# A written-out emission order made anew, with quarter matmuls side by side

## The chip, the cores and the metric

The program runs on one core of a Trainium2 chip. The metric is the device time of one execution in microseconds (us); lower is better. The engines of the core run side by side, each through its own list of instructions in order: PE (TensorE matmuls; PEld is its weight loads), DVE (VectorE), ACT (ScalarE), POOL (GpSimd), and SP (SyncE), which here issues every DMA.

## What is computed

The reference, cut to its core: attention with keys and values averaged over groups of eight tokens, then a gated MLP whose gate mixes tokens. There are 8 batches of 8 heads, 576 tokens and 64 channels a head; the model has 512 channels and a hidden width of 1024.

```python
k_p = k.reshape(B, H, 72, 8, D).mean(axis=3)
v_p = v.reshape(B, H, 72, 8, D).mean(axis=3)
scores = scale * q @ k_p.transpose(0, 1, 3, 2)
attn = softmax(scores)                       # over 72 pooled keys
x = (attn @ v_p) -> (B, S, H * D)
h = relu(x @ w_in); u, v = h[..., :512], h[..., 512:]
v_n = (v - mean(v)) / sqrt(var(v) + 1e-6)
v_s = einsum('ts,bsd->btd', w_spatial, v_n) + b_spatial[:, None]
out = (u * v_s) @ w_out
```

## The kernel before

Everything is done batch by batch, and every batch is cut into named steps. Attention has K and V (load and pool keys and values), KT (transpose the pooled keys), W (split the left-over pooled values into two parts), Q0 to Q3 (load and transpose the queries of a pair of heads), S0 to S3 (scores and softmax of such a pair), T0, T1, Y0, Y1 (move the probabilities so that pooled keys lie on partitions; Y is the last 64 tokens), and A00 to A11 (probabilities times values: the first digit is a half of the tokens, the second a half of the heads). The MLP has v0 to v4 (one token tile of the gate's input, with its normalisation), u00 to u13, s00 to s13 (token mixing and gating) and o0 to o4 (output projection). w steps load and split the weights. All operands of the large matmuls are split into a high and a low part, so each product takes three matmuls.

The scores (line 612) and the products with the values (line 751) are quarter matmuls: 64 rows by 64 columns of the array, four of which lie beside one another. The MLP's matmuls (lines 804, 820, 847, 865 to 867, 891) take the whole array. Line 754 adds the left-over values behind line 751.

No queue decides the order at run time. Each step is a Python generator; the string ORDER names a step, and `next` runs it to its next `yield`. A digit is the batch, `^`, `~`, `!` and `%` choose the engines of some operations of a step:

```python
for name in ORDER.split():
    ...
    next(parts[key], None)
```

Every engine, SP included, then works through its instructions in that order. Buffers come from rings: PSUM tiles "mm" and "tp" share one ring of four banks, the scores "s" have two, staging "kv" three. A step that takes a tile waits until the last user of that buffer has released it.

Places that the prediction speaks of: `softmax` (line 572 mx, 574 scaled mx, 588 exponentials on ACT, 595 the division on POOL); `load_f64` (lines 213, 222, 224, 227 on DVE, 230, 245, 247 on POOL), which splits a 64-bit weight block; `att_values` (line 504 vr_s) and `att_values_split` (line 512 vr); `normalise` (785 to 793, with the power at 791 on POOL); `moe_v` (808, 814 vn_l on POOL, 827, 837); `moe_s` (870 g, 876, 879 gT on POOL).

Of the kernel before, what the change touches and what calls it, by code (L numbers as in the profile page):

```python
# [23 lines left out]


ORDER = (
    "0Q1^~ 0Q1 wv3^ wv3 0Q1 wv3 0Q0^~ wv3 0Q0 0Q0 ws1 ws1 wv3 ws1 ws1 ws1 0K~ 0K 0V^ 0K 0K 0K 0K 0K 0S0 0S0 0S1 wv3 "
    "wv3 0S0 0S1 0S0 0S1 0S1 0S1 0K 0S0 0V 0S1 0V 0V 0V 0V 0V wv1 0K wv1 wv1 ws1 0S1 0Q2^ 0Q2 0Q2 0S2~ 0S2 0S0 wo1~ "
    "0W 0Y0 wv1 wv1 wv1 0Y0 0Q3^~ 0Y0 0Y0 0T0! 0T0 0T0 0T0 0T0 wo1 0W 0Q3 0Q3 0T0 0T0 0S2 wo1 1Q1^~ wo1 1K 1Q1 1K "
    "wv0~^ 0S3~ 0S3 1Q0^~ 0S2 1K wv2~ 0A00 0A00 0A00 0A00 0A00 1K 1V^ 1Q1 1V 1K 1K 1Q0 wv1 wv0 1Q0 1K 1S1~ wv0 0S3 "  # L30
    "0A10 0A10 1K 0S3 1S0~ wu2 0A10 0S2 wv0 wv0 0S3 0A10 0A10 wv2 1K wv0 0T1! 0S3 0T1 wv2 0Y1 0T1 0T1 0T1 0T1 0T1 "
    "wv2 0Y1 1S1 0Y1 wo1 wo1 0Y1 1V 1V 0A01 0A01 0A01 0A01 0A01 wv2 wv2 wu2 1V 1V wu3~ wu3 wu2 wu2 wu2 1V wu2 wu2 "
    "wu3 wu3 wu3 0v1 0A11 0v1 0A11 0v1 0A11 wu3 wu0 wu0 0A11 wu0 wu0 wb wb 2K~ wu1~^ 0v0 wu1 0v0 wu0 wu0 0A11 0v3 "
    "0v1 wu1 0v3 0v3 1Q2 0v3 1S0 ws4 0v1 1Q2 ws4 1Q3 0v4 ws4 wu0 ws4 0v2 ws4 ws4 0v0 0v0 1S1 1S1 1S1 2K 1S2~ 1S2 2K "
    "wu1 1Q3 0v4 0v4 1S0 0v0 wu1 wu1 wb 0u12 0v2 1S2 0v0 0v2 1S3 0v4 1S0 0u12 0u03 0v1 0u10 0u10 0u02 0v3 1S0 0u03 "
    "0v3 ws0 1T0! 2K 2K 1T0 0u02 0v2 2K 1S3 1T0 1T0 1T0 1T0 0u11 0v2 ws0 1T0 0v2 ws0 0v4 ws0 2Q0 ws0 2Q0 0v2 0u11 1W "
    "1W 0u13 2KT 2KT 0u00 2KT 0u13 0v4 0v4 0u00 1S3 2Q1 2Q1 ws0 1S3 0v0 2S0~ 1A00 2S0 0v3 0u01 0v1 1A00 1A00 1A00 "
    "1A00 1S1 0u01 1S3 ws3 0v4 0v4 ws3 ws3 1Y0 2S1 ws3 ws3 ws3 wo2~!% 1Y0 1Y0 1S3 0s01 wo2 1Y0 1A10 1A10 ws2 1S2 "
    "0s02 0s01 0s01 1A10 1A10 1A10 1S2 1T1! 1T1 1T1 0s01 0s02 1T1 1T1 1T1 wo2 2Q2 0s00 0s02 0s02 ws2 ws2 1T1 2Q2 "
    "0s03 wo3 ws2 0s03 0s03 2Q3 ws2 ws2 wo2 0s13 2S1 0s12 1S3 2S0 0s03 1Y1! wo2 0s00 wo2 2Q3 2S3 1Y1 1Y1 0s13 1Y1 "  # L40
    "2S1 1A11 0s12 1A11 1A11 1A11 3K! 3K 3K 1A11 1v3 1v3 3K wo2 0s12 3Q1 1A01 2S2 2S2 2S2 1A01 1A01 1A01 3K 0s00 3Q0 "
    "3Q0 wo2 2V! 3K 0s12 2S0 1A01 2S1 2S0 0s11 2S2 0s10 2S1 2S1 0s10 0s10 0s10 3KT wo3 1v0 1v0 wo3 wo3 wo3 wo0 0s13 "
    "2S2 0s11 2T0 2T0 0s11 3Q1 0s11 2T0 1u13 wo0 0s13 2S2 1u00 1u00 3Q2 1v2 wo0 wo0 1v2 1v2 3KT 3KT wo0 wo0 wo0 1v4 "
    "1v0 1u01 1u01 1v0 3S1~ 1v0 2T0 2T0 2T0 4Q0 3S1 1v4 1v4 1v4 1v4 wo3 0s00 wo3 1v2 1v2 2S3 2S3 1u10 1u13 1u03 1u10 "
    "1u03 2S1 2Y0! 2V 2Y0 0o3 2T0 2T0 1v1 2V 2V 2V 2S3 2S3 1v3 1v3 3S1 2Y0 1u12 1v3 0o0 1v3 1v1 1v1 0o0 2S3 1v3 0o0 "
    "3S0~ 1u11 0o3 1u11 1v0 2T1! 0o1 2T1 3Q2 3V~ 2T1 1v1 2T1 1v4 1v1 2V 2Y0 2Y0 2S3 2W 2W 2Y1! 1u12 1v1 2A10 2A10 "
    "2A10 0o1 2A10 2A10 3V 1v2 3V 1u02 2Y1 2A00 2A00 2A00 2T1 2T1 1v4 2A00 2A00 0o2 1v0 1v1 1v4 3S0 1v4 1v2 1s13 "
    "1s13 1s11 1s10 3S2~ 1s11 1s13 2Y1 1s12 3V 3V 3V 3S0 3S0 3S0 4Q0 1s10 1s13 0o1 1u02 3S2 1s00 0o2 2T1 1s12 4K! "
    "0o3 2T1 3S2 1s12 4K 4K 4K 1s12 4K 2A01 2A01 2A01 2A01 1s00 1s10 1s10 2A01 2Y1 2v1 2v1 2Y1 2A11 2A11 2A11 2A11 "
    "3Q3 3Q3 2v0 5K! 3S3 2A11 3T0 2v0 3T0 4K 4KT 1s00 1s00 3S1 3W 2v4 2v4 2v4 4Q1 4V~ 2v4 4V 1s01 4KT 1s01 3S1 1s01 "  # L50
    "3S3 1s02 3S1 1s02 3Y0 3Y0 4KT 3S3 1s11 1s11 1s03 4S0~ 1s03 3S3 3S3 2v1 1s02 2v1 1s02 2v1 1o4 1o4 1o2 3Y0 3S2 "
    "0o2 3S2 3T1 1o4 3W 1o2 2v4 3S3 4V 4V 2v4 4V 3Y0 3Y0 1s03 2u00 2u00 4Q1 4Q3 3T0 4Q2 2v1 2v3 2v3 2v3 2u13 2v3 4V "
    "3T0 3T0 2u11 3T0 4Q2 2v4 2u02 2v0 2v0 3T1 5Q0 2u13 2u11 2u01 2v4 2u12 2u12 4S0 4S0 2u03 2u03 2v1 1s01 4S1~ 4S1 "
    "5V~ 1s03 4S1 1o0 1o0 3T0 5K 1o2 2u01 2u02 1o3 1o3 4Q3 2v0 2v0 2v2 3T0 4S0 4S0 4T0 3T1 4T0 2v0 5K 5K 4S2 3S3 "
    "3Y1! 3T1 3T1 3T1 3A00 3A00 3A00 3A00 4S3 2v2 2v3 4S2 2v3 2v3 3Y1 2v2 2v2 3A00 3A10 2u10 3A10 1o3 2v2 2v2 2v2 "
    "2v4 3A10 3A10 3A10 4S1 4S1 1o1 4S2 2s10 5K 5K 4S2 3T1 2s01 2u10 2s10 2s10 2s10 5Q0 2s11 3Y1 1o0 2s11 2s11 2s02 "
    "5KT 1o1 2s02 6V~ 5Q2 4T0 3Y1 3Y1 2s01 4S1 2s01 4Y0 3T1 2s01 4T0 5KT 2s13 4T0 3A11 5KT 2s13 2s13 2s13 3A11 3A11 "
    "2s03 2s03 3A11 3A11 4S3 4S3 5Q2 3v2 4Y0 4Y0 2s03 3A01 3A01 3A01 3u11 6Q0 4S3 4S3 2s11 3A01 3A01 3v4 3v4 3v4 "
    "2s00 2s00 2s00 2s00 3v2 3v2 2s02 3v2 3v0 3v0 3v0 4S2 4S2 4T1 4S3 2s12 5S2~ 2s03 3v3 3u01 5Q3 5Q3 4W 3v2 2s12 "
# [907 lines left out]
```

## Time and profile before

| | |
|---|---|
| median of 3 runs | 576.53 us (573.49 to 578.07) |
| the profiled execution's own time | 573.28 us |
| its span, first to last instruction | 571.5 us |
| mean granted TensorE clock | 0.988 |
| PE, PEld busy | 94%, 80% of the span |
| DVE, ACT, POOL busy | 58%, 47%, 51% |
| chain that ended last | PE 67%, DVE 15%, ACT 5%, POOL 4%, DMA 4%, issue 3% |

The chain is followed back from the last instruction: at each point it shows the engine that everything behind it waited for. A matmul is shown with its whole passage through the array, so matmuls that follow one another overlap in the profile; what one costs is the distance from its start to the next one's start.

### The profile page before, as it was taken

Reading aid. Unit: us, or ns where it says so; the run is one execution under the profiler, and the core shown is the slowest. Engines: PE = TensorE matmul, PEld = TensorE weight load, DVE = VectorE, ACT = ScalarE, POOL = GpSimd, SP = SyncE. Lnnn points to the kernel's source line nnn. Section 1 sums busy time; section 2 is a strip of 40 time slices with the busy share of each in tenths; the row PEclk is TensorE's granted clock in tenths of the full one; section 3 lists DMA queues with packets and bytes.
Section 4 is the critical chain, followed back from the end, with each engine's and each line's share of the span. In section 5 each row is a group of like instructions: output and inputs, shape, how many; then the busy total and the mean of one; then the engine's idle time right before and its main releaser. Section 6 shows DMA issues by size and latency. Waiting matters only on the chain.

```text
span 571.5 us, 12170 instructions
## 1 busy us (share of the span) xinstructions
PE 538.1 (94%) x4514; PEld 456.3 (80%) x4514; DVE 333.0 (58%) x723; ACT 269.7 (47%) x875; POOL 288.9 (51%) x389
## 2 busy tenths in 40 slices
PE   4879798998999999999999999999999997999997
PEld 3666497887877896888888988988898895888996
DVE  3899999767864655566755655452845464333110
ACT  2675876543555426334564346425445333224231
POOL 2446555689776483834846645271544182132430
PEclk9999999999899999999999999999999998999999
DMA  8887155266167466445434342552134122001002
GB/s 224 244 278 166 46 123 100 81 118 154 48 183 181 120 125 170 149 115 121 115 105 122 111 97 98 115 146 58 62 103 128 44 87 72 24 2 51 24 25 87
DMA packets 124363, 63.13 MB, mean 110 GB/s; under 512 B 82960, under 2 KB 108048, under 8 KB 124304
## 3 DMA queue, kind: packets, MB, share of 16 engines
q1 hardware_dynamic: 124304, 62.36, 41.0%
q8 instruction: 35, 0.57, 0.4%
q14 instruction: 24, 0.20, 0.1%
HBM read 44.92 MB, written 17.40 MB: 109 GB/s over the span
## 4 chain that ended last, share of the span: by engine, by line
PE 67%; DVE 15%; ACT 5%; POOL 4%; DMA 4%; issue 3%; SPq 1%; DVEq 0%; ACTq 0%; POOLq 0%
PE mm L865 16%; PE mm L891 13%; PE mm L804 11%; PE mm L847 11%; PE tp L751 3%; PE s_ps L612 3%; ACT e L588 2%; PE tp L754 2%; PE mm L820 2%; DVE vv L793 1%; PE mm L866 1%; PE mm L867 1%; DVE x L222 1%; DVE vr_s L504 1%; DVE x L213 1%
## 5 line engine op out<-in xcount | busy, mean ns | idle before, releaser
L847 PE MATMUL mm<-xT,win_h 128*128 128x256 f32 (+1 forms) x512 | 104.3, 298 | 0.0
L879 POOL TENSOR_TENSOR gT<-g,gT 128x256 fp32r<-128x256 f32 x64 | 47.9, 753 | 99.0 <-ACT gT L876 91.3
L891 PE MATMUL mm<-wout_h,gT 128*128 128x512 f32 (+1 forms) x264 | 84.1, 401 | 3.2 <-DVE vv L827 2.7
L804 PE MATMUL mm<-win_h,xT 128*128 128x512 f32 x256 | 82.7, 402 | 4.3 <-DVE xT L183 2.4
L847 PEld LDWEIGHTS mm<-xT,win_h 128*128 128x128 f32 x512 | 83.6, 189 | 2.3
L865 PE MATMUL mm<-wT_h,vn_h 128*128 128x256 f32 (+1 forms) x256 | 76.4, 298 | 1.1 <-DVE xT L761 1.1
L847 PE MATMUL mm<-xT,win_l 128*128 128x256 f32 (+1 forms) x256 | 75.7, 296 | 0.0
L865 PE MATMUL mm<-wT_l,vn_h 128*128 128x256 f32 (+1 forms) x256 | 75.4, 295 | 0.0
L865 PE MATMUL mm<-wT_h,vn_l 128*128 128x256 f32 (+1 forms) x256 | 75.3, 294 | 0.0
L595 POOL TENSOR_TENSOR e<-e,rs 128x720 f32<-128x720 f32 (+1 forms) x32 | 41.8, 1305 | 51.9 <-DVE rs L593 46.5
L870 DVE TENSOR_TENSOR g<-mm,ru 128x256 f32<-128x256 f32 (+1 forms) x64 | 28.6, 451 | 62.2 <-PE mm L867 49.2
L891 PEld LDWEIGHTS mm<-wout_h,gT 128*128 128x128 f32 x264 | 49.6, 194 | 15.2 <-issue 2.9
L804 PEld LDWEIGHTS mm<-win_h,xT 128*128 128x128 f32 x256 | 46.6, 189 | 16.5 <-DVE xT L183 3.6
L791 POOL TENSOR_TENSOR rstd<-rstd,neg_half 128x1 f32<-128x1 f32 (+1 forms) x40 | 23.8, 598 | 66.2 <-DVE rstd L789 63.4
L588 ACT ACTIVATE e<-s_ps,mx 128x72 f32<-128x72 f32 x174 | 52.8, 334 | 7.2 <-DVE mx L574 7.0
L891 PE MATMUL mm<-wout_l,gT 128*128 128x512 f32 (+1 forms) x132 | 52.6, 399 | 0.0
L814 POOL TENSOR_TENSOR vn_l<-vv,vn_h 128x512 fp32r<-128x512 f32 x32 | 41.3, 1306 | 21.5 <-ACT vn_h L812 21.5
L804 PE MATMUL mm<-win_l,xT 128*128 128x512 f32 x128 | 50.6, 395 | 0.0
L307 POOL TENSOR_TENSOR st<-st 128x512 f32<-128x512 f32 (+1 forms) x44 | 46.9, 1065 | 6.6 <-DMA st<-in_k 4.1
L865 PEld LDWEIGHTS mm<-wT_h,vn_h 128*128 128x128 f32 x256 | 48.1, 188 | 2.5 <-issue 1.5
L876 ACT ACTIVATE gT<-g 128x256 fp32r<-128x256 f32 x64 | 26.3, 416 | 50.3 <-DVE g L870 50.1
L865 PEld LDWEIGHTS mm<-wT_h,vn_l 128*128 128x128 f32 x256 | 48.2, 188 | 0.4
(171 smaller groups left out, 1137.4 us busy)
## 6 DMA issues: line engine op xcount, KB each, us to landing
st<-in_k SPq DMA_DIRECT2D x32, 256.0 KB, 3.6
out<-ob SPq DMA_DIRECT2D x31, 256.0 KB, 2.1
qt<-in_q SPq DMA_DIRECT2D x104, 72.0 KB, 2.7
st<-in_v SPq DMA_DIRECT2D x48, 128.0 KB, 2.9
xd<-X SPq DMA_DIRECT2D x24, 256.0 KB, 3.0
pt<-xd SPq DMA_DIRECT2D x48, 128.0 KB, 2.8
stw<-in_moe_w_in SPq DMA_DIRECT2D x8, 512.0 KB, 6.5
st<-in_v SPq DMA_DIRECT2D x8, 256.0 KB, 5.2
```

The lines of the kernel that those rows point to most:

```text
L307: eng.tensor_tensor(st[:, :, :w], st[:, :, :w], st[:, :, w:2 * w], op=ALU.add)
L588: nc.scalar.activation(em[:, h, :], sv[:, h % 2, h // 2, :], AF.Exp, bias=mx[:, h:h + 1], scale=QK, accum_out=sm[:, h:h + 1])
L595: nc.gpsimd.tensor_tensor(em, em, rs.unsqueeze(2).broadcast_to([P, n, SP]), op=ALU.mult)
L791: nc.gpsimd.tensor_tensor(rstd[:m], rstd[:m], neg_half[:m], op=ALU.pow)
L804: nc.tensor.matmul(a, lhsT=xT[:, i, o + c * P:o + (c + 1) * P], rhs=w[:, i, DH:], start=(i == 0 and j == 0), stop=(i == NK - 1 and j == 2))
L814: nc.gpsimd.tensor_tensor(t["vn_l"][:, c, :], vv, f32(t["vn_h"][:, c, :]), op=ALU.subtract)
L847: nc.tensor.matmul(a, lhsT=w[:, i, d * P:(d + 1) * P], rhs=xT[:, i, o + ts.start:o + ts.stop], start=(i == 0 and j == 0), stop=(i == NK - ...
L865: nc.tensor.matmul(a, lhsT=x[:, c, ds], rhs=y[:, c, ts], start=(c == 0 and j == 0), stop=False)
L870: nc.vector.tensor_tensor(g, a, t["ru"][:, d, ts], op=ALU.mult)
L876: nc.scalar.activation(dst[:, d, 0, at:at + m], g[:, o:o + m], AF.Copy)
L879: nc.gpsimd.tensor_tensor(dst[:, d, 1, at:at + m], g[:, o:o + m], f32(dst[:, d, 0, at:at + m]), op=ALU.subtract)
L891: nc.tensor.matmul(a, lhsT=src[:, i, x, at:at + m], rhs=w[:, i, cols], start=(i == 0 and j == 0), stop=(i == ND - 1 and j == 2))
```

## The change

Only the string ORDER is replaced. The steps, their instructions, the shapes and the buffers are the same; each engine gets them in another order. The letters that choose engines are the same too.

```diff
 ORDER = (
-    "0Q1^~ 0Q1 wv3^ wv3 0Q1 wv3 0Q0^~ wv3 0Q0 0Q0 ws1 ws1 wv3 ws1 ws1 ws1 0K~ 0K 0V^ 0K 0K 0K 0K 0K 0S0 0S0 0S1 wv3 "
...
+    "ws1 ws1 0Q1^~ 0Q1 ws1 ws1 0Q1 wv3^ wv3 wv3 wv3 wv1 0Q0^~ wv3 wv1 0K~ 0Q0 wv1 wv1 wv1 wv1 0Q0 wv1 0K 0K 0K 0K 0K "
...
 )
```

What the order becomes on the engines is shown at three places. A factor at a row's end is the number of such instructions in a row.

First PE, in batch 1, at two of its score steps (S0 and S1; L847 is a step u of batch 0, L239 to L241 belong to a weight load). Before, each score step (16 or 16 + 4 rows of quarter matmuls) stands alone between whole-array work:

```order
L804 MATMUL mm<-win_l,xT 128x512
L612 MATMUL s_ps<-kT,qT 64x72 x16
L239 MATMUL mm<-x,ident 128x512
...
L847 MATMUL mm<-xT,win_l 128x320
L612 MATMUL s_ps<-kT,qT 64x72 x16
L612 MATMUL s_ps<-kT,pt_q 64x72 x4
L847 MATMUL mm<-xT,win_h 128x256 x2
```

In the changed order two score steps of the same batch and a product with values stand in one piece:

```order
L847 MATMUL mm<-xT,win_l 128x256
L612 MATMUL s_ps<-kT,qT 64x72 x32
L612 MATMUL s_ps<-kT,pt_q 64x72 x4
L751 MATMUL tp<-pt,vp 64x256 x4
L754 MATMUL tp<-pt_rr,vr 128x256 x2
L709 MATMUL tp<-ident,e 64x64 x4
```

Two steps of quarter matmuls that were apart are now neighbours. Over the whole of PE's list behind the first step v4 (line 820), the places where a score step meets another score step or a product with values are 9 before and 22 after: two score steps together 1 and 6, a score step next to a product 8 and 16.

Second POOL and DVE in batch 7, where the pooled values are split (steps V and W; vq is the last sum of V on POOL, and vr_s and vr on DVE wait for it). Before, POOL has three subtractions vn_l in a row right behind vq:

```order
L312 TENSOR_TENSOR vq<-st_r 64x64
L814 TENSOR_TENSOR vn_l<-vv,vn_h 128x512 x3
L879 TENSOR_TENSOR gT<-g,gT 128x256
```

and DVE at the same place:

```order
L793 TENSOR_SCALAR vv<-vv,mv,rstd 64x512
L504 TENSOR_TENSOR vr_s<-vq,mask 32x256 x2
L512 TENSOR_TENSOR vr<-vr_s,vr 32x512
L837 TENSOR_TENSOR vt<-vv,vt 64x512
```

In the changed order POOL's next work behind vq is two powers rstd, whose inputs DVE makes only behind vr:

```order
L312 TENSOR_TENSOR vq<-st_r 64x64
L791 TENSOR_TENSOR rstd<-rstd,neg_half 128x1 x2
L879 TENSOR_TENSOR gT<-g,gT 128x256
L814 TENSOR_TENSOR vn_l<-vv,vn_h 128x512
```

```order
L504 TENSOR_TENSOR vr_s<-vq,mask 32x256 x2
L512 TENSOR_TENSOR vr<-vr_s,vr 32x512
L676 STREAM_TRANSPOSE X<-e 128x512
L680 STREAM_TRANSPOSE XR<-pt_p 128x128
L785 BN_STATS st_6116<-vv 128x6
```

The values' split moved ahead of the normalisations of its batch and away from the run of vn_l.

Third SP at the start, where DMAs are issued for the first attention steps and the first weights (stw is a 64-bit block of w_in). Before:

```order
L528 DMA qt<-in_q 128x4x64 x2
L197 DMA stw<-in_moe_w_in 128x1024
L528 DMA qt<-in_q 128x4x64 x2
L531 DMA qt<-in_q 64x2x64 x2
L287 DMA st<-in_moe_w_spatial 128x576
L353 DMA st<-in_k 128x2x256 x2
L366 DMA st_r<-in_k 64x1x256 x2
```

and in the changed order:

```order
L287 DMA st<-in_moe_w_spatial 128x576
L528 DMA qt<-in_q 128x4x64 x2
L197 DMA stw<-in_moe_w_in 128x1024 x2
L528 DMA qt<-in_q 128x4x64 x2
L531 DMA qt<-in_q 64x2x64 x2
L353 DMA st<-in_k 128x2x256 x2
L366 DMA st_r<-in_k 64x1x256 x2
```

A second block of w_in now goes out ahead of the first keys, and the block of w_spatial goes out first of all.

## Rows read from the trace of the kernel before

**Rows 1.** The page: busy time of each engine, and GB/s moved by DMA in 40 equal slices of the span.

```profile
PE 538.1 (94%) x4514; PEld 456.3 (80%) x4514; DVE 333.0 (58%) x723; ACT 269.7 (47%) x875; POOL 288.9 (51%) x389
GB/s 224 244 278 166 46 123 100 81 118 154 48 183 181 120 125 170 149 115 121 115 105 122 111 97 98 115 146 58 62 103 128 44 87 72 24 2 51 24 25 87
```

**Rows 2.** The stretches of 20 us: start and end, length, busy us (and instructions) of PE, PEld, DVE, ACT, POOL, granted clock, DMA share, GB/s.

```profile
20.00:40.00 20.00, 15.18 (x326) 11.83 (x324) 19.03 (x44) 16.95 (x65) 10.38 (x13) 1.00 0.82 251
40.00:60.00 20.00, 17.61 (x134) 12.06 (x132) 19.04 (x29) 12.07 (x27) 13.46 (x12) 1.00 0.65 165
60.00:80.00 20.00, 17.20 (x152) 13.80 (x153) 19.32 (x40) 15.25 (x69) 11.46 (x14) 0.91 0.29 68
80.00:100.00 20.00, 18.07 (x226) 15.81 (x226) 17.97 (x35) 12.94 (x33) 10.76 (x15) 1.00 0.56 124
```

**Rows 3.** PE's instructions in order of time (start, us, what), around a score step alone, around two together, from a score step with a product behind it to the next score step, and from a product alone to the next step.

```profile
263.50 0.31 PE L867 MATMUL mm<-wT_l,vb 128*128 128x320 f32 x1
263.74 0.73 PE L612 MATMUL s_ps<-kT,qT 64*64 64x72 f32 x32
264.40 0.73 PE L804 MATMUL mm<-win_h,xT 128*128 128x512 f32 x2
264.97 0.40 PE L804 MATMUL mm<-win_l,xT 128*128 128x512 f32 x1
...
332.86 0.28 PE L847 MATMUL mm<-xT,win_l 128*128 128x256 f32 x1
333.07 1.23 PE L612 MATMUL s_ps<-kT,qT 64*64 64x72 f32 x64
...
334.36 0.74 PE L804 MATMUL mm<-win_h,xT 128*128 128x512 f32 x2
...
227.50 0.73 PE L612 MATMUL s_ps<-kT,qT 64*64 64x72 f32 x32
...
229.03 0.73 PE L612 MATMUL s_ps<-kT,qT 64*64 64x72 f32 x32
...
410.21 0.66 PE L751 MATMUL tp<-pt,vp 64*64 64x256 f32 x8
...
411.14 0.46 PE L847 MATMUL mm<-xT,win_h 128*128 128x320 f32 x2
```

**Rows 4.** One line's instructions over the whole span: count, then shortest, median and longest in ns.

```profile
L213 DVE TENSOR_SCALAR x<-x x12: 417/462/1401, 7.8 to 130.7; 128x512 uint32<-128x512 uint32 x12
L504 DVE TENSOR_TENSOR vr_s<-vq,mask x16: 361/414/3978, 22.2 to 475.2; 32x256 f32<-32x256 f32 x16
L512 DVE TENSOR_TENSOR vr<-vr_s,vr x8: 681/924/3607, 28.1 to 476.4; 32x512 fp32r<-32x512 f32 x8
L574 DVE TENSOR_SCALAR mx<-mx x20: 170/268/1206, 26.5 to 423.1; 128x8 f32<-128x8 f32 x13, 128x10 f32<-128x10 f32 x7
```

**Rows 5.** DVE's groups in the stretch from 20 to 100 us: count, busy us, mean ns of one, idle before.

```profile
L213 DVE TENSOR_SCALAR x<-x 128x512 uint32<-128x512 uint32 x8 | 7.4, 928 | 0.2
L512 DVE TENSOR_TENSOR vr<-vr_s,vr 32x512 fp32r<-32x512 f32 x2 | 4.4, 2187 | 0.0
L574 DVE TENSOR_SCALAR mx<-mx 128x8 f32<-128x8 f32 x4 | 3.0, 757 | 0.1
```

**Rows 6.** POOL's and DVE's instructions in order of time at batch 7's pooled values, and at batch 1's.

```profile
471.18 3.77 POOL L814 TENSOR_TENSOR vn_l<-vv,vn_h 128x512 fp32r<-128x512 f32 x3
...
471.25 4.41 DVE L504 TENSOR_TENSOR vr_s<-vq,mask 32x256 f32<-32x256 f32 x2 [0.75 <-POOL vq L312]
...
86.23 3.76 POOL L814 TENSOR_TENSOR vn_l<-vv,vn_h 128x512 fp32r<-128x512 f32 x3
...
86.93 3.61 DVE L512 TENSOR_TENSOR vr<-vr_s,vr 32x512 fp32r<-32x512 f32 x1
```

**Rows 7.** Pieces of the chain that ended last (start, us, what).

```profile
7.81 4.84 DMA st_r<-in_k
13.95 0.98 PE s_ps L612 x33
...
137.86 1.51 DVE vv L793
...
141.94 5.46 PE mm L891 x12
...
152.28 2.80 PE mm L891 x12
...
261.75 1.76 PE mm L865 x12
```

**Rows 8.** Who waited for whom: total us, times, longest.

```profile
PE mm L891 <- DVE vv L827: 2.7, 1, 2.7
PE tp L751 <- ACT ru L850: 2.7, 1, 2.7
PE tp L754 <- DVE vr L512: 1.2, 1, 1.2
```

**Rows 9.** A stretch behind batch 7's pooled values, as in rows 2.

```profile
477.50:481.50 4.00, 3.62 (x13) 2.08 (x14) 1.67 (x5) 2.24 (x6) 0.00 (x0) 0.70 0.25 87
```

**Rows 10.** Around two softmaxes that follow each other on ACT: PE's first output matmul behind the score step, and its first step behind the two output steps.

```profile
217.19 0.73 PE L891 MATMUL mm<-wout_h,gT 128*128 128x512 f32 x2
...
224.51 0.73 PE L804 MATMUL mm<-win_h,xT 128*128 128x512 f32 x2 [0.44 <-ACT ob L895]
```

128 rows, old and new, of the table ORDER are left out of this document.

## Prediction

> **What bounds the kernel now.** I read the page's busy times first. PE is busy 94% of the span [rows 1], and the chain that ended last lies 67% on it, so an engine other than PE matters only where PE waits for it. Then the stretches: from 20 to 100 us PE stands idle 4.8 + 2.4 + 2.8 + 1.9 = 11.9 us, while DVE is busy 19.0, 19.0, 19.3 and 18.0 of each 20 us [rows 2]. That is the start, where the first attention steps and the splitting of the weights all pass DVE, and DVE sets the pace there. Behind it PE is nearly full, and what can go is of two kinds: time that PE's own order costs it, and a few waits.
>
> The busy share hides both. A matmul is drawn with its passage, so the cost of a step is read from start to start. A score step of 32 quarter matmuls alone: the whole-array matmul ahead of it starts at 263.50 and at its full rate (12 in 1.76 us) lets the next one start 0.15 us later, but the score step starts at 263.74, 0.09 late; it holds PE until 264.40, 0.66; and the first two matmuls behind it take 0.57 to the third's start, against 0.46 at the full rate of 2.80 us for 12 [rows 3, 7], 0.10 more. So it costs 0.86 us, of which 0.19 are for going in and out.
>
> **Part 1, quarter matmuls side by side.** Two score steps together, of 32 and 40 quarter matmuls, run from 333.07 to 334.36, 1.29 us [rows 3]; with 0.09 ahead and 0.10 behind that is 1.48. Apart, the smaller is 0.86 and the larger, by its count, 0.19 + 0.66 x 40 / 32 = 1.01 (an estimate), 1.87 together. A meeting saves 0.39. For a score step with a product behind it: from 227.50 to 229.03, 1.53 us, and it already pays for the way into the next score step, so about 1.53 with its own 0.09 and without that [rows 3]. Apart it is 0.86 for the score step and 411.14 - 410.21 = 0.93 with 0.09 ahead for the product, 1.88. That saves 0.35. I take 0.36. Behind the first step v4 there are 22 meetings in the changed order and 9 before, so 13 x 0.36 = **-4.7 us**. All of it is on PE, where PE sets the end, and needs no cover. The ends: none if PE waits there anyway (0), all of it at 0.39 (-5.1).
>
> **Part 2, the start.** Some DVE operations take far longer than their shortest. The shift of a weight block (line 213) takes 417 ns at best [rows 4] and 928 on the mean of the eight from 20 to 100 us [rows 5]: 8 x 0.51 = 4.1 us. The split of the pooled values (line 512) takes 681 at best, 2187 on the mean of two: 3.0 us. The scaled maximum (line 574) takes 170 at best, 757 on the mean of four: 2.3 us. Together 9.4 us on an engine that has nothing to spare. What they have in common is that they read and write SBUF alone, and that POOL was at work: the 3.61 us of line 512 at 86.93 lie inside three subtractions vn_l that POOL ran from 86.23 to 89.99 [rows 6]. If the new order puts such work where POOL is idle, that time goes. How much of it cannot be read from an order, since it tells no times: the ends are 0 and 9.4. I take two thirds, 6.3, for a reason from the place shown in batch 7: the run of three vn_l behind vq is gone there, but POOL is busy over half of the time from 20 to 100 us [rows 2], so not all can be kept apart.
>
> Against it stands a cost. One more block of w_in goes out ahead of the first keys, 128 x 1024 words of 4 bytes, 0.52 MB. In the first two slices DMA moved 224 and 244 GB/s [rows 1], so the keys land 2.1 to 2.3 us later than now, where the last piece lands at 12.65 and the first scores start at 13.95 [rows 7]. Its ends are 0 (DVE does that block's work while it waits, and has it done later) and 2.3; I take 2.2, since the first scores hang on the keys. Net **-4.1 us**, from -9.4 to +2.3.
>
> **Part 3, waits behind the start.** Three of PE's waits have a DVE operation of that kind just ahead. At 139 us PE waits 2.7 us for DVE (line 827) [rows 8]; the normalisation ahead of it (line 793) took 1.51 us [rows 7]. The wait costs twice: the 12 output matmuls that follow take 5.46 us against 2.80 for such a dozen [rows 7], the clock at its lower level of 1.2 GHz after PE stood still, 2.7 more. Sum 5.4. At 474 us PE waits 2.7 us [rows 8], named ACT, because ACT's queue waits for vr_s, which DVE held for 3.98 us [rows 4] inside three vn_l [rows 6]; in the 4.0 us behind it the granted clock is 0.70 [rows 9], 1.2 lost. Sum 3.9. At 89 us PE waits 1.2 us for line 512 [rows 8]. In all 10.5 us. The same two thirds: **-7.0 us**, from 0 to -10.5. What is late next at those places is POOL's own chain, which the change leaves at about the same length; DVE's operation then ends 1 to 3 us earlier, which is as much as each wait.
>
> At batch 7 the rows show a DVE operation that lost to three POOL instructions in a row: 3.98 us for work of 0.36 [rows 4], and line 512 the same, 3.61 for 0.68 [rows 4, 6]. The Trainium skill, page "SBUF — State Buffer", section "Who interferes with whom", says that a DVE instruction with two SBUF inputs and a POOL instruction that reads SBUF exclude each other, and that the loser waits for the whole instruction of the other. Taken strictly that is one vn_l, 3.77 / 3 = 1.26 us; here no order of issue let DVE in between, and the trace goes beyond the page.
>
> **Part 4, softmaxes in pairs.** Two score steps together send two softmaxes to ACT at once; there are 6 such pairs behind the start against 1. The pair that stands in the trace is followed by the next step at once [rows 3]: 0. Where two softmaxes follow each other on ACT, from 217.19 to 224.51, 24 output matmuls hold PE 7.3 us against 5.6, because PSUM tiles wait for ACT [rows 7, 10]: 1.7. I take 0.4, near the row of the same thing: 5 x 0.4 = **+2.0 us**, from 0 to +8.5.
>
> Everything else (the late batches, the tail, the DMAs of q, k and v) moves by a few places on engines that are busy half of the time or less, and is set at nothing; its cover is PE's own work, and if that cover is gone a wait as in part 3 is the price.
>
> **The sum.** -4.7 - 4.1 - 7.0 + 2.0 = -13.8 us. Against the profiled execution's 573.3 that is 559.5; it was 3.2 us below the median, so against the median of 576.5 it is **563 us**, 2.4% faster.
>
> **The rivals.** *The waits only move (575 us).* An operation that is held back in its list until POOL is idle waits as long as one that waits at SBUF. DVE and POOL are busy 58% and 51% of the span [rows 1], and in the start DVE has no idle time in which to shift anything, which speaks for it; the batch 7 place, where vr_s now meets an idle POOL, speaks against. Then -4.7 for part 1, +2.2 for the keys and about +1 for pairs: 575. Chance 0.22.
>
> *Paired softmaxes hold PSUM (585 us).* The place is each pair: 20 to 40 exponentials on ACT ahead of the copies that empty PSUM, PE held on the ring of four banks. At 1.7 us a pair it is 5 x 1.7 = 8.5, with one drop of the clock at 2.7, the keys 2.2, less 4.7: +8.7, 585. With nothing gained at POOL, the change is slower by more than 1% from (5.8 + 4.7 - 2.2) / 5 = 1.7 us a pair; a pair in the trace without any wait speaks against it. Chance 0.12.
>
> *Only one instruction's wait is in reach (565 us).* If of the waits at vr_s and vr only one vn_l is due to POOL, 1.26 of 3.6 us [rows 4, 6], then of 3.9 + 1.2 = 5.1 us in part 3 only 1.8 can go, part 3 is two thirds of 7.2, 4.8, and the time 565. This is the rule of the Trainium skill's page above, as a mechanism of this kernel. Chance 0.08, since POOL's three subtractions and DVE's wait end together.
>
> **How the numbers follow.** The forecast has 0.58. It and the last rival lie more than 1% below, 0.66 faster; 0.22 within 1%; 0.12 slower. 1% is about what a measurement of this kernel can tell from no change, since its three runs spread by 0.8%. With every part at its best end the sum is -5.1 - 9.4 - 10.5 = -25.0, 552; upward the range takes in the rival that the waits only move and stops short of the slow one: 552 to 578.
>
> **What would show it.** PE's busy time falls by about 5 us with as many matmuls; the transitions of line 612 into 751 stand without a late start. The longest of lines 504 and 512 falls from 4.0 and 3.6 us to below 1.5, the mean of 213 from 20 to 100 us below 0.7. The waits at 139, 474 and 89 us have no like of over 2 us, and the mean clock rises above 0.988. First scores start near 16 us. I am wrong if new PE waits of some 2 us each stand behind paired score steps, or if DVE's busy time stays near 333 us: then nothing was kept apart.

## The result and the profile after

The changed kernel takes **546.5 us**, median of 4 runs (545.3 to 546.8), against 575.9 for the kernel before in the same series (4 runs, 573.5 to 578.1). The ratio is 0.949, with a 95% interval of 0.944 to 0.953: 5.1% faster, 29.4 us. The forecast was 13.8 us, with a range that ended at 552. The sign was right; the size forecast was under half of what came.

The page of the changed kernel, its busy line and the granted clock in 40 slices; then the stretches of 20 us, with columns as in [rows 2]:

```profile
PE 524.1 (96%) x4514; PEld 451.7 (83%) x4514; DVE 321.9 (59%) x723; ACT 269.0 (49%) x875; POOL 287.3 (53%) x389
PEclk9999999999999999999999999999999999999999
...
20.00:40.00 20.00, 16.80 (x274) 11.83 (x272) 17.77 (x39) 16.71 (x66) 6.82 (x13) 1.00 0.86 248
40.00:60.00 20.00, 19.77 (x218) 15.29 (x218) 18.70 (x36) 16.62 (x62) 10.30 (x8) 1.00 0.78 197
60.00:80.00 20.00, 19.63 (x207) 17.16 (x206) 19.13 (x47) 15.37 (x45) 16.03 (x20) 1.00 0.58 125
80.00:100.00 20.00, 19.14 (x279) 16.35 (x277) 17.57 (x37) 14.89 (x52) 16.16 (x18) 1.00 0.27 62
```

The span is 545.0 us against 571.5. DVE, ACT and POOL run as many instructions as before [rows 1]; DVE is busy 11 us less. PE stands idle 545.0 - 524.1 = 20.9 us against 33.4, and from 20 to 100 us 4.7 against 11.9 [rows 2]. Its clock is at the upper level, 2.4 GHz, throughout. That does not hang on one execution: the mean granted clock is 0.997 to 1.000 in the four runs of the changed kernel, and 0.979 to 0.991 in all runs of the kernel before in the later series.

The two places at which PE had waited longest behind the start, 139 us and 474 us, as stretches of before and then the stretches of after in which the same work lies (same columns):

```profile
130.00:150.00 20.00, 17.31 (x115) 14.54 (x114) 15.49 (x32) 9.73 (x36) 17.78 (x21) 0.83 0.52 131
470.00:490.00 20.00, 16.95 (x92) 13.27 (x91) 8.91 (x13) 7.26 (x18) 5.81 (x8) 0.91 0.23 67
```

```profile
125.00:145.00 20.00, 20.00 (x171) 16.99 (x169) 15.73 (x38) 11.30 (x36) 16.89 (x24) 1.00 0.52 160
440.00:460.00 20.00, 20.00 (x117) 18.03 (x116) 5.72 (x13) 6.77 (x14) 5.72 (x6) 1.00 0.30 95
```

PE's idle time and the low clock are both gone. The longest waits of after, over the whole span; the first, second and fourth lie in its first 31 us:

```profile
PE tp L545 <- DMA qt<-in_q: 6.0, 3, 4.5
PE mm L292 <- DMA st<-in_moe_w_spatial: 3.9, 1, 3.9
PE tp L754 <- DVE pt_rr L640: 1.9, 2, 1.0
PE tp L709 <- ACT pt L663: 1.5, 1, 1.5
```

DVE's operations that had lost time, shortest, median and longest as in [rows 4]:

```profile
L504 DVE TENSOR_TENSOR vr_s<-vq,mask x16: 406/444/1597, 24.0 to 428.3; 32x256 f32<-32x256 f32 x16
L512 DVE TENSOR_TENSOR vr<-vr_s,vr x8: 681/682/1720, 27.4 to 429.4; 32x512 fp32r<-32x512 f32 x8
```

and the groups from 20 to 100 us as in [rows 5]:

```profile
L213 DVE TENSOR_SCALAR x<-x 128x512 uint32<-128x512 uint32 x8 | 4.0, 502 | 0.1
L574 DVE TENSOR_SCALAR mx<-mx 128x8 f32<-128x8 f32 x4 | 2.0, 505 | 0.1
L512 DVE TENSOR_TENSOR vr<-vr_s,vr 32x512 fp32r<-32x512 f32 x2 | 1.4, 682 | 0.1
```

The longest fell from 3978 and 3607 ns (the forecast was below 1500), the means from 928, 757 and 2187.

**Where PE's time went.** I took, for every matmul behind 90 us, the distance to the next start less the median distance for its line and shape, and added up these excesses. Steps into, out of and within quarter matmuls: 29.7 us before, 25.5 after, -4.2. Whole-array matmuls behind one another, excess under 0.4 us each: 7.8 and 1.0, -6.8. Single gaps of 0.4 us and more: 13.6 and 4.4, -9.2. Together -20.1 of the 26.5 us by which the two spans differ; 6.4 lie ahead of 90 us. The choice of the median moves each of these sums by some 0.3 us. The lower clock level makes up most of the second sum, but not all of it: behind 90 us of before the granted clock is 0.50 (1.2 GHz) for 6.8 us from 141.2 and for 3.4 us from 479.1, which at half speed is at most 5.1 us lost (an estimate). The gaps at 139 and 474 us and what follows them up to the end of these stretches make 11 of the 16.0 us of the last two sums.

### The profile page after: what moved, and what is told of

Same layout as the page of the kernel before. It is cut to its first block, busy times and chain, and to the rows that moved or that the text cites. A ratio compares the mean times of both kernels' runs of the same rounds, so it can differ in the third digit from the quotient of the medians.

```text
span 545.0 us, 12145 instructions
## 1 busy us (share of the span) xinstructions
PE 524.1 (96%) x4514; PEld 451.7 (83%) x4514; DVE 321.9 (59%) x723; ACT 269.0 (49%) x875; POOL 287.3 (53%) x389
## 4 chain that ended last, share of the span: by engine, by line
PE 72%; DVE 7%; SPq 7%; DMA 4%; ACT 4%; POOL 3%; issue 3%; DVEq 0%; ACTq 0%; POOLq 0%
PE mm L865 15%; PE mm L891 15%; PE mm L847 13%; PE mm L804 13%; PE s_ps L612 3%; PE tp L751 2%; PE tp L754 2%; PE mm L820 2%; DMA qt<-in_q 2%; SPq L735 1%; PE mm L867 1%; PE mm L866 1%; SPq L692 1%; DMA pt_r<-xdlr 1%; POOL vn_l L814 1%
## 5 line engine op out<-in xcount | busy, mean ns | idle before, releaser
L847 PE MATMUL mm<-xT,win_h 128*128 128x256 f32 (+1 forms) x512 | 103.6, 296 | 0.5 <-ACT ob L895 0.4
L847 PEld LDWEIGHTS mm<-xT,win_h 128*128 128x128 f32 x512 | 83.5, 188 | 3.3 <-ACT ob L895 0.7
L891 PE MATMUL mm<-wout_h,gT 128*128 128x512 f32 (+1 forms) x264 | 81.1, 389 | 0.0
L804 PE MATMUL mm<-win_h,xT 128*128 128x512 f32 x256 | 81.0, 397 | 0.0
L865 PE MATMUL mm<-wT_h,vn_h 128*128 128x320 f32 (+1 forms) x256 | 76.3, 298 | 0.0
L847 PE MATMUL mm<-xT,win_l 128*128 128x256 f32 (+1 forms) x256 | 75.6, 295 | 0.0
L865 PE MATMUL mm<-wT_h,vn_l 128*128 128x320 f32 (+1 forms) x256 | 75.5, 295 | 0.0
L865 PE MATMUL mm<-wT_l,vn_h 128*128 128x320 f32 (+1 forms) x256 | 75.4, 294 | 0.0
L891 PEld LDWEIGHTS mm<-wout_h,gT 128*128 128x128 f32 x264 | 48.2, 188 | 10.7 <-POOL gT L879 0.7
L891 PE MATMUL mm<-wout_l,gT 128*128 128x512 f32 (+1 forms) x132 | 51.4, 390 | 0.0
L847 PEld LDWEIGHTS mm<-xT,win_l 128*128 128x128 f32 x256 | 48.2, 188 | 0.0
```

The source lines that it names most:

```text
L804: nc.tensor.matmul(a, lhsT=xT[:, i, o + c * P:o + (c + 1) * P], rhs=w[:, i, DH:], start=(i == 0 and j == 0), stop=(i == NK - 1 and j == 2))
L847: nc.tensor.matmul(a, lhsT=w[:, i, d * P:(d + 1) * P], rhs=xT[:, i, o + ts.start:o + ts.stop], start=(i == 0 and j == 0), stop=(i == NK - ...
L865: nc.tensor.matmul(a, lhsT=x[:, c, ds], rhs=y[:, c, ts], start=(c == 0 and j == 0), stop=False)
L891: nc.tensor.matmul(a, lhsT=src[:, i, x, at:at + m], rhs=w[:, i, cols], start=(i == 0 and j == 0), stop=(i == ND - 1 and j == 2))
```

## The experiments

### Where in the order the gain lies

The changed kernel was not run again beside the experiments. Its 546.5 us are from the first series, where the kernel before took 575.9; in the later series the kernel before took 573.5 to 575.0 (medians). So differences of 1 to 2 us from the changed kernel are not resolved.

Four splices. One order is taken to a cut; behind it the other order follows, less what has been called. Two cut at the end of the start, two later, where the engines' lists part at some 171 us (changed order first) and 186 us (order of before first).

```diff
 ORDER = (
-    (all 1660 names of before, or of the changed order)
+    (the first 160, 155 or 605 names of one order)
+    (the names of the other order, in its sequence, without those already called)
 )
```

> The first 160 calls in the changed order (up to the first step v of batch 0), all that follow in the order of before. If the start was undersized in my sum (there -4.1 us), this keeps what the changed trace is ahead by where PE has done its first 70 us of matmuls, 88.1 - 82.3 = 5.8 us, so 6 to 9 us faster than before, 567 to 570. If what the start gains is given back as soon as the old order follows, 574 to 577.

> The other way round: the first 155 calls in the order of before, all that follow in the changed order. If start and rest add up, the rest alone is worth 29.4 - 6 to 9, so 20 to 23 us faster than before, 553 to 556. If the start is worth only the 4.1 us of my sum, 551. If nearly all of the gain hangs on the start, 565 or more.

> The first 605 calls in the changed order (to about 195 us of the trace of before), the rest in the order of before. Where PE has done 160 us of matmuls the changed trace is 15.6 us ahead. If that lasts: 15 to 16 us faster than before, 558 to 560. If part of it is given back where the old order follows, as in the splice at the start, 562 to 568.

> The first 605 calls in the order of before, the rest in the changed order. By the traces 26.7 - 15.6 = 11.1 us are gained behind there: 563 to 565. By the terms of my prediction only the wait at 474 us (3.9) and some ten meetings (3.6) lie there: 567 to 569.

Measured against before: new_start 571.6 us, 0.995 (0.992 to 0.998), 2.8 us faster; old_start 550.3 us, 3.8 slower than the changed kernel; early_605 557.3 us, 0.970 (0.967 to 0.972), 17.4 faster; late_605 570.4 us, 0.993 (0.991 to 0.995), 4.1 faster. new_start lies between its two expectations, old_start just below the 551 of my sum, early_605 0.7 us below what was expected of it. So the start is worth **3 to 4 us**, though the two traces differ by 6.4 us ahead of 90 us. One pair of traces misleads there: from 20 to 30 and from 30 to 40 us the trace of before has a granted clock of 1.00, while old_start and late_605, which have the same start, have 0.83 and 0.89. The changed kernel's trace shows 1.00 there. So a part of the 3 to 4 us may be low clock, which my sum for the start does not have; no run separates it.

The two later splices give 17.4 + 4.1 = 21.5, not 29.4. Each splice has a wait at its seam. The longest wait at the cut in late_605, then in early_605:

```profile
PE tp L451 <- POOL kr L312: 4.1, 1, 4.1
```

```profile
PE mm L804 <- DVE g L870: 2.9, 1, 2.9
```

Neither order has these waits, and together they are 7.0 us of the 7.9 that are missing. late_605 missed both its expectations, by 1.4 and 5.4 us, with 4.1 of wait at the seam; its wait at batch 7's values is gone, as in the changed kernel.

### Quarter steps taken apart

The edit moves 13 whole-array steps, one more than the expectation counts. One of the 13 places (3u10 is a whole-array step, 5S1 and 4A10 are quarter steps):

```diff
-    5S1~ 5S1 4A10 4T1 2o2 6K 4T1 6K 3u10 4A10
+    5S1~ 5S1 3u10 4A10 4T1 2o2 6K 4T1 6K 4A10
```

> The changed order with a step of whole-array matmuls put between the two quarter-matmul steps of 12 meetings (10 are left of 22, before had 9). By part 1 of the prediction 12 x 0.36 = 4.3 us slower than the changed kernel, 551. If a meeting saves nothing, or if softmaxes in pairs cost what a meeting saves, 546 to 547.

Measured: 560.1 us, 13.5 slower than the changed kernel: three times the theory's price. PE's list in the trace has 9 meetings of the 22 left. By the account above, 3.1 us of the loss are steps into and out of quarter matmuls, 3.1 / 13 = 0.24 a meeting; most of the rest is new waits (gaps of 0.4 us and more: 12.4 against 4.4). Two such waits in apart:

```profile
244.48 0.73 PE L804 MATMUL mm<-win_h,xT 128*128 128x512 f32 x2 [0.81 <-DVE xT L183]
...
295.89 0.94 PE L612 MATMUL s_ps<-kT,qT 64*64 64x72 f32 x32 [2.22 <-DVE pt_q L558]
```

A product with values that is followed at once by the step that reads its result waits for DVE to empty PSUM; a score step that comes early waits for its queries. So the time of apart prices more than meetings. By its account a meeting is worth somewhat less than part 1 said, and the place of a step against its inputs is worth more.

### Two waits, moved by hand

In w7_early three calls of batch 7 (the last of V, and W) move ahead, so that vr_s and vr no longer meet the three vn_l. In rstd_first two powers rstd of batch 1 (calls 1v0 and 1v2) move ahead of a wout block's split in POOL's list.

```diff
 w7_early, in the order of before:
-    7V 6u01 6u01 6u12 ... 6v4 6v4 6u02 7V 7W 6u02 7W 5o4
+    7V 7V 7W 7W 6u01 6u01 6u12 ... 6v4 6v4 6u02 6u02 5o4
 rstd_first, in the order of before:
-    wo0 wo0 wo0 1v4 1v0 1u01 1u01 1v0 ... wo3 1v2 1v2
+    wo0 1v0 1v0 1v2 wo0 wo0 1v4 1u01 1u01 ... wo3 1v2
```

> The order of before with one move: the last call of V and the two of W of batch 7 go 21 calls ahead, so that POOL makes vq, and DVE vr_s and vr, before POOL's three subtractions vn_l and not behind and beside them. PE's order is the same. If DVE's loss to POOL is what made PE wait at 474 us, 2.7 us of wait and 1.2 of low clock go, up to the 5.4 by which the changed trace gains there: 3.9 to 5.4 faster, 570 to 572, and vr_s at 0.4 us an instruction. If the wait only moves (to vn_l, to the operands of the next products), 575 to 577.

> The order of before with one move: two powers rstd of batch 1 stand ahead of the split of a wout block in POOL's list, and not behind it; PE's order is the same. Fills in place of vn_l left the wait at 139 us as it was, so the theory now is that there DVE waits for rstd in POOL's list (2.6 us), not at SBUF. Then the wait of 2.7 us falls to about 0.7 (ACT's copy for the next step still waits for wout_l, which comes 1.1 us later), and with it the low clock behind it where that shows (2.7): 2 to 4.7 us faster than before, 570 to 573. If the loss of line 793 and 574 beside POOL sets it, or the wait only moves, within 1 us, 574 to 576.

**w7_early** is slower: 1.0046 (1.0027 to 1.0064), 2.6 us, as expected for a wait that only moves. DVE, POOL and PE in w7_early:

```profile
466.64 0.84 DVE L504 TENSOR_TENSOR vr_s<-vq,mask 32x256 f32<-32x256 f32 x2 [2.79 <-POOL vq L312]
...
474.61 3.95 DVE L793 TENSOR_SCALAR vv<-vv,mv,rstd 64x512 f32<-64x512 f32 x1 [0.66 <-POOL rstd L791]
...
474.55 3.73 POOL L814 TENSOR_TENSOR vn_l<-vv,vn_h 128x512 fp32r<-128x512 f32 x3
...
480.06 0.75 PE L751 MATMUL tp<-pt,vp 64*64 64x320 f32 x2 [3.53 <-ACT ru L850]
```

vr_s took 0.42 us each, as expected, and then the next SBUF-only operation of DVE, a normalisation, fell under the same three vn_l: 3.95 us instead of 0.5. ACT waits for it in its list, and PE for ACT. DVE's loss to the three vn_l was rightly named, but the wait only moved. The changed order takes the run itself apart; there the same two operations took this, at 428 us:

```profile
427.89 0.84 DVE L504 TENSOR_TENSOR vr_s<-vq,mask 32x256 f32<-32x256 f32 x2 [1.61 <-POOL vq L312]
429.43 0.68 DVE L512 TENSOR_TENSOR vr<-vr_s,vr 32x512 fp32r<-32x512 f32 x1 [0.70 <-ACT vr L510]
```

**rstd_first** is 0.997 (0.994 to 0.999), 1.9 us faster. What stood there in before, POOL and then DVE:

```profile
136.02 1.29 POOL L247 TENSOR_TENSOR wout_l<-x,y 128x512 fp32r<-128x512 f32 x1
137.26 0.56 POOL L791 TENSOR_TENSOR rstd<-rstd,neg_half 128x1 f32<-128x1 f32 x1
...
135.10 0.15 DVE L789 TENSOR_SCALAR rstd<-mv 128x1 f32<-128x1 f32 x1
137.86 1.51 DVE L793 TENSOR_SCALAR vv<-vv,mv,rstd 128x512 f32<-128x512 f32 x1 [2.60 <-POOL rstd L791]
140.22 0.98 DVE L574 TENSOR_SCALAR mx<-mx 128x10 f32<-128x10 f32 x1
```

and in rstd_first POOL, DVE and PE:

```profile
135.90 1.18 POOL L791 TENSOR_TENSOR rstd<-rstd,neg_half 128x1 f32<-128x1 f32 x2 [0.63 <-DVE rstd L789]
...
136.49 0.55 DVE L793 TENSOR_SCALAR vv<-vv,mv,rstd 128x512 f32<-128x512 f32 x1 [0.68 <-POOL rstd L791]
137.89 0.37 DVE L574 TENSOR_SCALAR mx<-mx 128x10 f32<-128x10 f32 x1
...
141.07 0.70 PE L891 MATMUL mm<-wout_h,gT 128*128 128x512 f32 x2 [1.24 <-DVE vv L827]
```

PE's wait fell from 2.7 to 1.2 us. At this place PE's excess fell from 5.9 us to 1.7, but 2.7 of the 5.9 are the low clock, which does not come in every execution (last section); the sure part is 1.5 us, near the 1.9 of the times. What I had put down to SBUF alone (1.51 us in line 793) begins in POOL's list: rstd stood behind three 1.3 us instructions of a weight split, and DVE waited 2.60 us for it, now 0.68. But the move also took lines 793 and 574 out from beside the weight split: they fell from 1.51 and 0.98 us to 0.55 and 0.37, 1.6 together. So rstd_first shows that POOL's order at this place costs PE 1.5 us; how much of that is waiting in the list and how much is loss at SBUF it does not separate.

### POOL without reads, and copies between

In fill_b (order of before) and fill_a (changed order) each vn_l is replaced by two fills and a short subtraction; together about as long (1.1 + 0.25 us against 1.3). In gap_b and gap_a vn_l stays, and a one-column copy that waits for it stands behind it.

```diff
 fill_b, fill_a:
-            nc.gpsimd.tensor_tensor(t["vn_l"][:, c, :], vv, f32(t["vn_h"][:, c, :]), op=ALU.subtract)
+            for _ in range(2): nc.gpsimd.memset(f32(t["vn_l"][:, c, :]), 0.0)
+            nc.gpsimd.tensor_tensor(t["vn_l"][:, c, :32], vv[:, :32], f32(t["vn_h"][:, c, :32]), op=ALU.subtract)
 gap_b, gap_a:
             nc.gpsimd.tensor_tensor(t["vn_l"][:, c, :], vv, f32(t["vn_h"][:, c, :]), op=ALU.subtract)
+            nc.gpsimd.tensor_copy(seen, f32(t["vn_l"][:, c, :1]))
```

> The order of before; in place of each subtraction vn_l POOL fills the block twice with zeros and subtracts 32 of its 512 columns, about as long (1.3 us), so that POOL reads next to no SBUF there. This leaves the low part of the gate's input out of 480 of 512 channels. If what PE loses behind the start in the order of before is DVE's loss to runs of vn_l, a good part of the some 16 us goes: 8 to 14 us faster than before, 561 to 567, and no normalisation (line 793) or vr_s above 1.7 us behind 130 us. If the order's own lateness is what PE waits for, within 2 us of before, 573 to 576.

> The same in the changed order, with the same part left out. If the changed order already keeps vn_l and DVE apart where it matters, at most 3 us faster than the changed kernel, 543.5 to 546.5. If both orders gain alike (8 us or more here too), what tells them apart is not this loss.

> The order of before, and behind each of the 32 subtractions vn_l a one-column POOL copy that reads its result and so waits for it; the computation is whole. It adds 32 x 0.25 = 8 us to POOL's busy time. If such a copy lets DVE in, the 3.98 and 3.61 us of lines 504 and 512 fall to about 1.6 and the waits at 474 and 89 us shrink: 3 to 6 us faster than before, 568 to 571; the rest of what the fills gained (10 us) was then vn_l's own time or single losses. If not, 574 to 577.

> The same copies in the changed order, which has few runs of vn_l left: within 2 us of the changed kernel, 545 to 548.5; below 545 it would be a version that beats both.

Measured: fill_b 565.0 us, 9.7 faster than before (574.7; ratio 0.982, 0.977 to 0.988); fill_a 545.0, 1.5 faster than the changed kernel. So what DVE loses beside vn_l costs the order of before about **8 us** more than the changed order (the interval of fill_b leaves 7 to 13 us for the 9.7, and the 1.5 of fill_a is not resolved). The wait at 139 us stayed in fill_b, where the weight split still runs, which sent me to POOL's list (the line number is one higher there):

```profile
PE mm L892 <- DVE vv L828: 2.7, 1, 2.7
```

gap_b is 0.995 (0.993 to 0.998), 3.2 us faster than before with the whole computation, at the low end of what was expected. DVE and POOL at batch 7 in gap_b:

```profile
468.34 3.08 DVE L504 TENSOR_TENSOR vr_s<-vq,mask 32x256 f32<-32x256 f32 x2 [0.75 <-POOL vq L312]
...
468.27 1.28 POOL L814 TENSOR_TENSOR vn_l<-vv,vn_h 128x512 fp32r<-128x512 f32 x1
469.62 0.27 POOL L815 COPY seen<-vn_l 128x1 f32<-128x1 f32 x1
469.85 1.29 POOL L814 TENSOR_TENSOR vn_l<-vv,vn_h 128x512 fp32r<-128x512 f32 x1
```

DVE gets in between two vn_l, and loses one of them for each of its two operations: 3.08 us for both against 4.41 [rows 6]. gap_a is 545.9 us, no different from the changed kernel. No version clearly beats it.

### The keys

```diff
 keys_first, the order of the DMAs in the changed kernel:
-    w_in block 1, w_in block 2 (wv1), q, keys, values
+    w_in block 1, q, keys, w_in block 2 (wv1), values
```

> The changed order with one DMA moved: the second block of w_in (wv1) goes out behind the first keys and not ahead of them; every other engine's order is the same. By the 2.2 us that my sum has for the later keys: first scores 2 us earlier and 544.3. If DVE does that block's work while it waits for the keys, and has it done for later, 546 to 548.

Measured: 550.6 us, 4.1 slower than the changed kernel, outside both expectations. The keys landed earlier, but DVE's list, which was the same, has the block's work ahead of the copies of the keys; DVE waited 6.6 us for the block:

```profile
16.40 0.43 DVE L213 TENSOR_SCALAR x<-x 128x512 uint32<-128x512 uint32 x1 [6.56 <-ACT x L208]
```

First scores came at 19.16 us, against 16.29 in the changed kernel. The experiment doesn't price the later keys; it shows that moving this DMA alone did not help while the list of the engine that reads it stayed the same.

### What DVE loses beside POOL

Four probes behind the last output of the kernel of before, each with DVE operations in the middle of POOL instructions. The lines of the first, with comments added:

```diff
+        nc.vector.tensor_copy(p[:, :2], a[:, :2])   # lets POOL start
+        beside()                                    # three POOL instructions, or five fills
+        nc.vector.tensor_reduce(small[:, 1:2], a, axis=AX.X, op=ALU.max)
+        op()                                        # the DVE operation that is measured
```

> The kernel of before with a probe behind its last output: five DVE operations (one SBUF input 128x512, two SBUF inputs, one of two inputs in PSUM, a 128x10 product, a maximum), each alone, then each beside three POOL subtractions with two SBUF inputs, beside three POOL products with one, and beside five fills. If SBUF-only DVE operations are shut out for a whole run of POOL instructions that read SBUF: about 3 us instead of 0.2 to 0.7 for the first, second and fourth beside both kinds of POOL reads, nothing lost for PSUM input and maximum, nothing beside the fills. [...]

> The kernel of before with a second probe behind its last output. Three DVE operations (128x512 with one SBUF input, 128x512 with two, 128x10 with one), each beside three POOL subtractions: in a chain through one block, as in the first probe; on three blocks that do not depend on each other, as a run of vn_l is; the same with a one-column fill after each; the same with a one-column copy after each. If a chain lets DVE in because POOL drains between its links: about 1 us for the first in the chain, 3 to 4 us on three blocks, as the 3.95 and 3.98 us in the traces, and whichever filler drains POOL brings it back to about 1. If DVE loses one POOL instruction only, about 1 us in all four, and the 3.95 us in the traces have another cause.

> The kernel of before with a third probe behind its last output: three DVE operations (128x512 with one SBUF input, 128x512 with two, 128x10 with one), each beside three POOL subtractions of which none waits for anything; then the first two again, with a one-column copy behind each subtraction that reads its output, and so waits for it. In the first two probes each POOL instruction had a wait, on DVE or on POOL itself. If DVE is shut out as long as POOL runs instructions without a wait between them: 3 to 3.9 us beside the run of three, about 1 with the copies. If a run without waits lets DVE in after one instruction as well: about 1 us throughout, and the 3.95 us stay unexplained.

> The kernel of before with a fourth probe behind its last output: three POOL subtractions exactly as vn_l (three inputs, rounded output, no wait between them), beside a DVE product of 128x512 with one SBUF input, of 64x512 with one, of 32x512 with two and of 32x256 with two; first without, then with a one-column copy behind each subtraction. If DVE operations on fewer partitions are shut out for the whole run: about 1 us for 128 partitions, 3 us and more for 64 and 32, and about 1 with the copies. If not, one POOL instruction (1 to 1.5 us) for all, and the 3.95 us stay open.

Rows of DVE in the first probe. Lines 969 to 973 are, in this order, a product with one SBUF input, with two, with one input in PSUM, a 128x10 product and a maximum. The first two rows are alone, the next five beside subtractions, the next beside POOL products with one input, the last beside fills:

```profile
568.24 0.43 DVE L969 TENSOR_SCALAR a<-a 128x512 f32<-128x512 f32 x1
569.65 0.68 DVE L970 TENSOR_TENSOR w<-a,w 128x512 f32<-128x512 f32 x1
...
575.61 1.07 DVE L969 TENSOR_SCALAR a<-a 128x512 f32<-128x512 f32 x1
580.05 1.45 DVE L970 TENSOR_TENSOR w<-a,w 128x512 f32<-128x512 f32 x1
584.87 0.68 DVE L971 TENSOR_TENSOR w<-mm,w 128x512 f32<-128x512 f32 x1
589.48 0.81 DVE L972 TENSOR_SCALAR small<-small 128x10 f32<-128x10 f32 x1
593.85 0.68 DVE L973 TENSOR_REDUCE small<-a 128x1 f32<-128x512 f32 x1
...
598.46 0.43 DVE L969 TENSOR_SCALAR a<-a 128x512 f32<-128x512 f32 x1
...
624.43 0.43 DVE L969 TENSOR_SCALAR a<-a 128x512 f32<-128x512 f32 x1
```

Operations with SBUF operands alone wait to the end of the POOL subtraction that is running, 0.6 to 0.8 us more here; an input in PSUM and the maximum lose nothing; POOL's fills and one-input products cost the one-input product nothing. In the other probes DVE lost one subtraction again: 1.31 us for two inputs on independent blocks, 1.57 without any wait between the subtractions, and with vn_l's own form 1.18 and 1.45 on 64 and 32 partitions. Each of my explanations for three lost subtractions in a row fell: a chain, a missing wait, the shape of DVE's operation. (In probe3 the first measured operation met a long fill instead of the subtractions.) Beside two vn_l in a row in the kernel itself, at 528.86 us of before, DVE also lost one only: line 793 took 1.51 us. In the changed kernel it lost more in one place: from 79.27 us line 793 took 2.23 us, over the end of a vn_l, a power rstd and a second vn_l. Why DVE lost all three at batch 7, 3.98 us in before and 3.97 again in early_605, **stays open**. The Trainium skill, page "SBUF — State Buffer", section "Who interferes with whom", says that whoever issues first has the shared pair for the whole instruction: beside one subtraction the probes agree, 1.07 against 0.43 us, beside POOL's one-input products nothing was lost, and the 3.98, 3.97 and 3.95 us in the kernel go beyond it.

## Why the prediction was wrong

**Part 1, meetings: right in size.** Forecast -4.7, measured -4.2 by the account, of which 0.8 lie at the stall at 474 us. Behind 90 us there are 20 meetings against 8, so this is 0.35 a meeting; apart gives 0.24. Assumed were 0.36.

**Part 2, the start: right in size.** Forecast -4.1; the splices give 3 to 4, a part of which may be low clock. The long operations of DVE fell as said: of 4.1 + 3.0 + 2.3 us of excess [rows 4, 5], 0.7 + 0 + 1.3 are left. First scores came at 16.29 us, 2.3 later, as said.

**Part 3, late waits: the step that failed.** Forecast -7.0; by the starts of PE's matmuls the three places gave some **-12.9** in the two traces, more than the -10.5 that the prediction had as this part's best end. Three things were wrong in it.
- The price. I took 10.5 us for the three places. By the starts PE lost some 5.9 at 139 us, 6.0 at 474 and 3.8 at 89, 15.7 in all; of these some 2.8 are left where the same work lies now. The place at 139 us was priced about right (5.4), the others were not (3.9 and 1.2). The waits as named leave out the shorter ones behind the first and the slow matmuls between.
- The factor of two thirds. It was carried over from the start. At these places 12.9 of 15.7 went.
- The cause at 139 us. I had it at SBUF alone. rstd_first shows that it hangs on POOL's list: DVE first waits for rstd behind the weight split, and then loses beside that split. The new order mends it too: DVE's longest wait for rstd fell from 2.6 us to 1.3.

A part of the 15.7 us belongs to one execution. Of the 5.9 us at 139 us 2.7 are low clock that other executions of before do not have there; they have it elsewhere, and the mean granted clock of before is below that of the changed kernel in every run.

**Part 4, pairs: nothing, where I had +2.0.** One of the six pairs in the changed kernel, and PE's next step:

```profile
130.25 1.23 PE L612 MATMUL s_ps<-kT,qT 64*64 64x72 f32 x64
131.30 0.30 PE L612 MATMUL s_ps<-kT,pt_q 64*64 64x72 f32 x8
131.53 0.73 PE L804 MATMUL mm<-win_h,xT 128*128 128x512 f32 x2
```

The others (84.3, 187.7, 220.2, 239.2 and 292.1 us) are followed at once too, and no wait of PE behind the start is over 1.0 us. By the starts three gaps of 1.1 to 1.4 us are left behind 90 us (150.5, 163.7 and 228.1 us), all between lines 751 and 754, where a product waits for its left-over operands: once for vr, which took DVE 1.66 us instead of 0.68, and twice for pt_rr behind a DMA of the probabilities. None waits for exponentials to free PSUM. The row of a pair stood in the trace of before; I should have gone by it.

**"Everything else" at nothing** was wrong as well, by less: the single gaps behind 90 us other than those at 139 and 474 us fell from 6.5 us to 4.4, and the small excesses away from these two places by some 3 us. Start 3 to 4, meetings 4.2, vn_l beside DVE 8 and POOL's list at 139 us 2 to 4 make 17 to 20 of the 29.4 us. These come from different measures and may overlap, and the other 9 to 12 us no run takes apart; their cause stays open.

Of the rivals, that the waits only move came true where I moved one place by hand (w7_early gained nothing), but not for the order as a whole. Paired softmaxes held nothing. That DVE loses one instruction only holds in the probes; as a bound on what the kernel could gain (565 us) it was too low.

## What to carry to other kernels

Price a wait by PE's starts from its beginning to the first matmul at full rate, not by the wait that is named: here the three places came out half as much again. Before you move an operation that a run of long GpSimd instructions holds up, look at what comes next in its engine's list, since that may fall under the run instead; taking the run apart helped here. And look in GpSimd's list for small instructions that others wait for.

## What the runs showed of the hardware

- DVE lost three POOL subtractions in a row in the kernel (3.95 to 3.98 us), and never more than one in the probes. The reason stays open.
- One POOL fill of 128x4096 (3.51 us) held a one-input DVE product of 0.43 us for 2.95, while five fills of 128x512 held it not at all. DVE, then POOL, in probe3:

```profile
570.53 2.95 DVE L967 TENSOR_SCALAR a<-a 128x512 f32<-128x512 f32 x1
...
569.69 3.51 POOL L950 MEMSET gT<- 128x4096 f32 x1
```

- The clock behind a stall is not certain. The same wait of 2.7 us at 139 us stands in before and in w7_early, and in the 8 us that begin with it the granted clock (the column behind POOL) is 0.63 in the one and 1.00 in the other; in late_605 it was 1.00 again, in fill_b 0.79. Before, then w7_early:

```profile
139.00:147.00 8.00, 5.31 (x15) 4.07 (x14) 7.10 (x14) 3.69 (x10) 7.35 (x9) 0.63 0.45 102
```

```profile
141.00:149.00 8.00, 5.32 (x26) 4.26 (x25) 7.13 (x13) 3.32 (x8) 7.46 (x9) 1.00 0.43 103
```

- POOL loses too: in probe4 its next subtraction, behind a two-input DVE product that got in, took 1.71 us instead of 1.26.
